# Decoding float64 weights in a fused attention and two-MLP kernel: signs on GpSimd, two VectorE passes in place of three

## The chip, the cores and the metric

The kernel runs on one core of a Trainium2 chip. The metric is device time in microseconds of one execution; lower is better. The core's engines work side by side, each through its own queue in order: TensorE (PE, matrix products into PSUM), VectorE (DVE), ScalarE (ACT), GpSimd (POOL) and SyncE (SP), which issues all the DMAs.

## The reference

Three parts follow each other, here in outline, for 2 sequences of 768 positions. Attention has 8 heads of 64, a causal window of 96 positions beside 8 global ones, and a distance bias. Its output, 512 wide, goes through an MLP with a convolution of 3 taps along the sequence as its gate, and then through an MLP with a spatial product over positions.

```python
x = attention(q, k, v, n_global, n_local)          # (2, 768, 512), fp32
h = relu(x @ w_in)                                 # 512 -> 1024, w_in: float64
h = h * sigmoid(conv3(h, conv_w))                  # conv_w: float64
x = h @ w_out                                      # 1024 -> 512, w_out: float64
h = relu(x @ w_in2)                                # 512 -> 1024, w_in2: float64
u, v = split(h, 2)
v = normalise(v)                                   # over the 512 columns
out = (u * (w_spatial @ v + b_spatial)) @ w_out2   # w_out2: float64
```

The weights w_in, conv_w, w_out, w_in2 and w_out2 are float64, as the scaling by a NumPy float64 in the inputs makes them. q, k, v and w_spatial are worked on as fp32.

## The kernel before

**Weights.** A weight is cut into blocks of 128 partitions by 512 columns: w1 (w_in) and w2 (w_out) have eight each, w3v and w3u (the two halves of w_in2) four each, w4 (w_out2) four. `split_jobs` (line 705) makes one job of a block: load its 512 KB of float64 as pairs of int32 words into a raw buffer (six of them for the first four weights), decode it to fp32 in a wk buffer (four of them), and split that with `parts` (line 558) into a high and a low fp16 half. The high half is a cast on ScalarE (line 496), the low half a subtraction on GpSimd or VectorE (line 510). Every product is then three matmuls of halves: high by high, high by low, low by high.

**Decoding.** `decode` (line 667) has four passes over a block, `hi` and `lo` being the two words of each float64. ScalarE (line 677) reads `hi` as an fp32 number and scales it, which moves the exponent into place. VectorE shifts the result left by three bits (line 684), ORs in the top three bits of `lo` (line 687), and ORs in the sign bit of `hi` (line 692). The convolution's taps, cwt, pass through the same function with 24 columns.

**Other work that bears on the change.** In the attention, line 842 (VectorE) takes scores out of PSUM with their bias and minimum, line 860 (ScalarE) takes the exponentials, line 855 (GpSimd) shifts the minima, and lines 496 and 510 split the probabilities into ph halves. `inner` (line 1034) does the first product (line 1050), relu (1392), the taps (1057, 1063), tanh (1083), the gate (1088) and the split into hh and hl. `outer` (line 1104) does the second product (line 1120) with w2's halves; its result ys is split by lines 494 and 506.

**Order.** The order is made when the kernel is built. `Plan` (line 105) holds every piece of work as a task with a cost for each engine that can do it, some with two engines to choose from, and what it reads and writes. `order` (line 150) lists the tasks by due times, then draws the due times anew `TRIES` times, with a spread, and keeps the shortest plan (lines 173 to 178). The instructions then stand on each engine in that order and can't overtake each other. Up to 70 us of the plan, dummy matmuls (`warm`, line 1019) fill TensorE's gaps. In the present order w1's blocks are decoded from 12 to 50 us, w2's from 50 to 100, w3v's and w3u's up to 160 and w4's around 290.

Of the kernel before, what the change touches and what calls it, by code (L numbers as in the profile page):

```python
# [9 lines left out]
F32 = mybir.dt.float32  # L10
# [4 lines left out]
I32 = mybir.dt.int32  # L15
I64 = mybir.dt.int64
U16 = mybir.dt.uint16
AF = mybir.ActivationFunctionType
ALU = mybir.AluOpType
# [22 lines left out]
VW = 2 * D + 2  # L42
OUT_LO = [0, 254, 510, S]

LEAD_TICKS, LEAD_STEPS = 12, 8

NATS, PLAINS = (0, 1, 2), (0, 1)
# [8 lines left out]

ROUNDS, SLACK, AHEAD, MARGIN, BIAS, CLOSE = 6, 0.5, 60.0, 1.0, 10.0, 15.0

TRIES, SPREAD = 150, 0.7

WARM_TO, WARM_AGAIN = 70.0, 8

# [13 lines left out]
def act(n):  # L76
    return 0.15 + 0.00085 * n
# [298 lines left out]
class Kernel:  # L376
# [287 lines left out]

    def decode(self, f, raw, reads, writes, by=1):

        nc, n = self.nc, f.shape[-1]
        lo, hi, fi = raw[:, :, 0], raw[:, :, 1], f.bitcast(I32)
        base = 2.0**-112 * 2.0 ** {1: 0, 256: 1}[by]

        def scale(e):
            if e == "ACT":
                nc.scalar.activation(out=f, in_=hi.bitcast(F32), func=AF.Copy, scale=base)
            else:
                nc.vector.tensor_scalar(
                    out=f, in0=hi.bitcast(F32), scalar1=base, scalar2=None, op0=ALU.mult  # L680
                )

        def shift(e):
            nc.vector.tensor_scalar(out=fi, in0=fi, scalar1=3, scalar2=None, op0=ALU.logical_shift_left)

        def low(e):
            nc.vector.scalar_tensor_tensor(
                out=fi, in0=lo, scalar=29, in1=fi, op0=ALU.logical_shift_right, op1=ALU.bitwise_or
            )

        def sign(e):
            nc.vector.scalar_tensor_tensor(  # L692
                out=fi, in0=hi, scalar=-(2**31), in1=fi, op0=ALU.bitwise_and, op1=ALU.bitwise_or
            )

        self.plan.add(dict(ACT=act(n)), scale, reads=reads, writes=writes)
        self.plan.add(dict(DVE=0.1 + 0.0008 * n), shift, reads=reads, writes=writes)
        for cost, e in ((0.0014, low), (0.0011, sign)):
            self.plan.add(dict(DVE=0.1 + cost * n), e, reads=reads, writes=writes)
# [5 lines left out]
    def split_jobs(self, weights, raw):  # L705

        jobs = []

        def job(kind, j, src):
            n = self.plan.next(raw)  # L710
            words = self.m(*n).bitcast(I32)
            self.load(words.bitcast(I64), src[:, j], [n], 8 * 512 * P)
            w = self.plan.next("wk")
            f = self.m(*w)[:, :512]
            hi, lo = (part[j] for part in self.blocks(kind))
            name = (kind, 0, j)
            self.decode(f, words.rearrange("p (n t) -> p n t", t=2), [n], [w], 2 ** self.k["w"])
            self.parts(512, hi, lo, f, [w], [(*name, "h")], [(*name, "l")])

        for kind, src in weights:  # L720
            for j in range(src.shape[1]):
                jobs.append(lambda args=(kind, j, src): job(*args))
        return jobs
# [1027 lines left out]
```

## Time and profile before

| | us |
|---|---|
| median of 3 runs | 383.51 |
| the runs | 378.37, 383.51, 384.13 |
| the profiled execution | 378.64 |
| its span, first to last instruction | 376.8 |

| engine | busy us | share of the span |
|---|---|---|
| TensorE | 357.0 | 95% |
| VectorE | 289.2 | 77% |
| ScalarE | 275.0 | 73% |
| GpSimd | 200.4 | 53% |

A busy share is a mean over stages with different limits, so the views that are read for the change are cut by stage. A busy TensorE is not one at its peak: matmuls overlap, and their ends are modelled. Its granted clock is given as a share of 2.4 GHz; the mean over the span is 0.978. Spans on GpSimd are rough.

### The profile page before, as it was taken

The numbers are of one execution on the slowest core, as the hardware profiler recorded it, in microseconds if no ns is written. First come the engines' busy times: TensorE is split into PE (matmuls) and PEld (weight loads), VectorE is DVE, ScalarE is ACT, GpSimd is POOL, SyncE is SP. The second block draws the span as 40 slices with busy tenths as digits, with TensorE's granted clock in tenths as the row PEclk, the third lists the DMA queues.
The fourth block names the chain that finished last, engine by engine and source line by source line (L and its number), as shares of the span: only waits on it lengthen the run. The fifth ranks groups of instructions, "written<-read, shape, count | busy, mean of one in ns | idle before, by whom it ended". The sixth has DMA issues, their size and how long they took to land.

```text
span 376.8 us, 8106 instructions
## 1 busy us (share of the span) xinstructions
PE 357.0 (95%) x2906; PEld 256.1 (68%) x2906; DVE 289.2 (77%) x745; ACT 275.0 (73%) x686; POOL 200.4 (53%) x287
## 2 busy tenths in 40 slices
PE   8999999995879999989999999999999999999994
PEld 5677987773778765666887879887545666664443
DVE  4689999997968898957886787799798897995000
ACT  3899989996737886768988895996788866555221
POOL 4341536759824479746948443779953699000000
PEclk9999999998699999989999999999999999999998
DMA  7966724976383413556422547000234000001222
GB/s 206 408 231 202 275 82 143 283 209 195 72 211 140 121 58 95 104 154 151 93 44 57 108 76 206 2 1 3 53 128 157 14 1 2 0 1 57 104 94 92
DMA packets 46258, 43.64 MB, mean 116 GB/s; under 512 B 34816, under 2 KB 36608, under 8 KB 45696
## 3 DMA queue, kind: packets, MB, share of 16 engines
q1 hardware_dynamic: 46208, 43.03, 40.3%
q8 instruction: 25, 0.41, 0.4%
q14 instruction: 25, 0.20, 0.2%
HBM read 31.48 MB, written 3.15 MB: 92 GB/s over the span
## 4 chain that ended last, share of the span: by engine, by line
PE 55%; DMA 2%; POOL 0%; ACT 0%; issue 0%; ACTq 0%
PE bank L1325 11%; PE bank L1120 9%; PE bank L1050 9%; PE bank L1475 8%; PE bank L1413 7%; PE bank L1204 6%; PE bank L823 2%; DMA pt_dt_float<-ph_dt_float 2%; PE bank L934 1%; PE bank L976 1%; PE bank L935 1%; PE bank L936 1%; PE bank L781 0%; POOL ph_dt_float L510 0%; POOL hl_dt_float L510 0%; ACT sb_dt_float L860 0%
## 5 line engine op out<-in xcount | busy, mean ns | idle before, releaser
L1050 PE MATMUL bank<-x_dt_float,w1h_dt_float 128*128 128x260 f16 (+1 forms) x384 | 64.8, 273 | 0.0
L1120 PE MATMUL bank<-hh_dt_float,w2l_dt_float 128*128 128x254 f16 (+2 forms) x192 | 53.9, 281 | 2.5 <-POOL w2l_dt_float L510 2.5
L1120 PE MATMUL bank<-hl_dt_float,w2h_dt_float 128*128 128x254 f16 (+2 forms) x192 | 53.9, 281 | 1.9 <-POOL hl_dt_float L510 1.2
L1120 PE MATMUL bank<-hh_dt_float,w2h_dt_float 128*128 128x254 f16 (+2 forms) x192 | 54.0, 281 | 1.2 <-DVE ys_dt_float L506 0.9
L1050 PE MATMUL bank<-x_dt_float,w1l_dt_float 128*128 128x260 f16 (+1 forms) x192 | 52.3, 273 | 0.0
L1063 DVE SCALAR_TENSOR_TENSOR bank<-hp_dt_float,cwt,bank 128x254 f32<-128x254 f32 (+2 forms) x96 | 45.7, 485 | 7.7 <-ACT bank L1057 4.9
L510 POOL TENSOR_TENSOR ph_dt_float<-sb_dt_float,ph_dt_float 128x512 f16<-128x512 f32 x30 | 36.3, 1211 | 21.2 <-ACT ph_dt_float L496 9.2
L510 POOL TENSOR_TENSOR hl_dt_float<-ac_dt_float,hh_dt_float 128x254 f16<-128x254 f32 (+2 forms) x47 | 34.2, 741 | 22.1 <-ACT hh_dt_float L496 16.2
L1120 PEld LDWEIGHTS <-w2h_dt_float 128*128 128x128 f16 x384 | 36.7, 100 | 9.5 <-issue 3.2
L842 DVE CUSTOM_DVE_ANT_0 sb_dt_float<-bank,bias_dt_float 128x256 f32<-128x256 f32 (+1 forms) x96 | 35.1, 400 | 9.1 <-PE bank L823 4.5
L1050 PEld LDWEIGHTS <-w1h_dt_float 128*128 128x128 f16 x384 | 36.9, 97 | 5.7 <-issue 0.7
L860 ACT ACTIVATE sb_dt_float<-sb_dt_float,nb_dt_float 128x256 f32<-128x256 f32 (+1 forms) x64 | 29.1, 492 | 3.9 <-POOL nb_dt_float L855 3.0
L1413 PE MATMUL bank<-ys_dt_float,w3uh_dt_float 128*128 128x384 f16 x128 | 31.2, 326 | 0.0
L1475 PE MATMUL bank<-w4h_dt_float,g_dt_float 128*128 128x512 f16 (+1 forms) x104 | 28.9, 363 | 0.0
L1204 PE MATMUL bank<-w3vh_dt_float,ys_dt_float 128*128 128x512 f16 x96 | 28.6, 379 | 0.0
L1475 PEld LDWEIGHTS <-g_dt_float 128*128 128x128 f16 x156 | 15.2, 98 | 15.8
L1325 PE MATMUL bank<-ws_dt_float,vn_dt_float 128*128 128x384 f16 x144 | 25.0, 326 | 0.0
L692 DVE SCALAR_TENSOR_TENSOR wk_dt_float<-raw_dt_float,wk_dt_float 128x512 int32<-128x512 int32 x28 | 24.9, 894 | 0.1
L1120 PEld LDWEIGHTS <-w2l_dt_float 128*128 128x128 f16 x192 | 19.3, 101 | 8.0 <-POOL w2l_dt_float L510 2.8
L1204 PEld LDWEIGHTS <-ys_dt_float 128*128 128x128 f16 x144 | 13.8, 98 | 15.8
L494 ACT ACTIVATE wk_dt_float<-bank 128x512 f32<-128x512 f32 (+1 forms) x13 | 7.3, 564 | 21.7 <-PE bank L1475 21.7
L1057 ACT ACTIVATE bank<-hp_dt_float,cwt 128x254 f32<-128x254 f32 (+2 forms) x48 | 22.5, 478 | 0.0
(186 smaller groups left out, 995.3 us busy)
## 6 DMA issues: line engine op xcount, KB each, us to landing
raw_dt_float<-in_w SPq DMA_DIRECT2D x20, 512.0 KB, 5.7
qk_dt_float<-in_qk SPq DMA_DIRECT2D x24, 336.0 KB, 3.4
v_dt_float<-in_vb SPq DMA_DIRECT2D x4, 1024.0 KB, 6.0
out_x<-wk_dt_float SPq DMA_DIRECT2D x11, 256.0 KB, 2.0
raw_dt_float<-in_wst SPq DMA_DIRECT2D x6, 384.0 KB, 3.7
raw_dt_float<-in_w3v SPq DMA_DIRECT2D x4, 512.0 KB, 4.3
raw_dt_float<-in_w3u SPq DMA_DIRECT2D x4, 512.0 KB, 3.8
v_dt_float<-in_vb SPq DMA_DIRECT2D x2, 768.0 KB, 6.2
```

What stands on the lines that cost most here:

```text
L510: self.engines[e].tensor_tensor(out=out, in0=in0, in1=in1, op=ALU.subtract)
L692: nc.vector.scalar_tensor_tensor(out=fi, in0=hi, scalar=-(2**31), in1=fi, op0=ALU.bitwise_and, op1=ALU.bitwise_or)
L842: nc.vector.tensor_tensor_reduce(out=sb[:, h, :n], in0=self.ps(self.sp[s][h])[:, :n], in1=self.m("bias", 2 * p + h)[:, t0 : t0 + n], scale ...
L860: nc.scalar.activation(out=sb[:, h, :n], in_=sb[:, h, :n], func=AF.Exp, scale=-1.0, bias=nb[:, h : h + 1])
L1050: nc.tensor.matmul(self.ps(acc)[:, :nx], w[f][:, k * P : (k + 1) * P], x[:, k, x0:], start=k == n == 0, stop=k == 3 and n == 2,)
L1057: nc.scalar.activation(out=ac(), in_=near(1), func=AF.Copy, scale=tap(1))
L1063: nc.vector.scalar_tensor_tensor(out=ac(), in0=near(j), scalar=tap(j), in1=ac(), op0=ALU.mult, op1=ALU.add)
L1120: nc.tensor.matmul(ps(), w[2 * d + k // 4][:, k % 4 * P : (k % 4 + 1) * P], x, start=k == n == 0, stop=k == 7 and n == 2,)
L1204: nc.tensor.matmul(ps(), x[:, y, k, tk], w[k], start=n == 0, stop=n == 11)
L1325: self.nc.tensor.matmul(self.ps(acc)[:, :HS], v[:, k, x, ek], w[:, k, y], start=n == 0, stop=n == 8)
L1413: nc.tensor.matmul(ps(), w[e4][:, k * P : (k + 1) * P], x[:, y, k, s], start=n == 0, stop=n == 11)
L1475: nc.tensor.matmul(ps(), x[:, y, k, tk], w[k][:, at], start=n == 0, stop=n == 11)
```

## The change

The blocks of w1, w2, w3v and w3u go through a new function, `decode_beside`. The pass of ScalarE stays. After it, GpSimd multiplies `hi` as fp32 by zero, in place, which leaves a zero with the sign of the number: a word with the sign bit alone. VectorE then has two passes instead of three. The first shifts `lo` right by 29 bits and ORs it with that word, in place of `lo`; the second shifts ScalarE's result left by three and ORs it with that. w4, cwt and the wide fallback keep the old function. The planner's number of draws goes from 150 to 60.

```diff
+BESIDE = ("w1", "w2", "w3v", "w3u")
...
-TRIES, SPREAD = 150, 0.7
+TRIES, SPREAD = 60, 0.7
...
+    def decode_beside(self, f, raw, reads, writes, by):
+        nc, n = self.nc, f.shape[-1]
+        lo, hi, fi = raw[:, :, 0], raw[:, :, 1], f.bitcast(I32)
+        base = 2.0**-112 * 2.0 ** {1: 0, 256: 1}[by]
+        size = hi.bitcast(F32)
+
+        def signs(e):
+            nc.gpsimd.tensor_scalar(out=size, in0=size, scalar1=0.0, scalar2=None, op0=ALU.mult)
+
+        def low(e):
+            nc.vector.scalar_tensor_tensor(
+                out=lo, in0=lo, scalar=29, in1=hi, op0=ALU.logical_shift_right, op1=ALU.bitwise_or
+            )
+
+        def joined(e):
+            nc.vector.scalar_tensor_tensor(
+                out=fi, in0=fi, scalar=3, in1=lo, op0=ALU.logical_shift_left, op1=ALU.bitwise_or
+            )
+
+        self.plan.add(
+            dict(ACT=act(n)), lambda e: nc.scalar.activation(out=f, in_=size, func=AF.Copy, scale=base), reads=reads,
+            writes=writes,
+        )
+        self.plan.add(dict(POOL=0.2 + 0.0019 * n), signs, writes=reads)
+        self.plan.add(dict(DVE=0.1 + 0.0014 * n), low, writes=reads)
+        self.plan.add(dict(DVE=0.1 + 0.0012 * n), joined, reads=reads, writes=writes)
...
-            self.decode(f, words.rearrange("p (n t) -> p n t", t=2), [n], [w], 2 ** self.k["w"])
+            decode = self.decode_beside if kind in BESIDE and self.half else self.decode
+            decode(f, words.rearrange("p (n t) -> p n t", t=2), [n], [w], 2 ** self.k["w"])
```

## Rows read from the trace of the kernel before

**Rows 1.** The page: busy us, share, instructions of each engine; then the dummy matmuls.
```profile
PE 357.0 (95%) x2906; PEld 256.1 (68%) x2906; DVE 289.2 (77%) x745; ACT 275.0 (73%) x686; POOL 200.4 (53%) x287
...
L1021 PE MATMUL bank<-hl_dt_float 128*128 128x256 f16 x84 | 12.9, 299 | 1.2 <-DVE hl_dt_float L578 1.2
```

**Rows 2.** Windows by stage: busy us and instructions of each engine, TensorE's granted clock.
```profile
core 0: us, PE busy (x) PEld busy (x) DVE busy (x) ACT busy (x) POOL busy (x), PEclk, DMA share, GB/s
...
10.00:50.00 40.00, 38.63 (x305) 31.77 (x303) 34.74 (x115) 35.56 (x86) 14.46 (x20) 1.00 0.73 264
50.00:84.00 34.00, 33.48 (x283) 26.76 (x281) 32.56 (x93) 32.21 (x84) 20.97 (x29) 1.00 0.68 188
84.00:105.00 21.00, 14.78 (x143) 11.65 (x142) 17.57 (x31) 15.37 (x37) 18.47 (x19) 0.76 0.54 142
105.00:160.00 55.00, 51.67 (x484) 38.21 (x481) 46.16 (x120) 39.04 (x93) 34.41 (x49) 1.00 0.46 118
...
170.00:285.00 115.00, 114.57 (x1073) 87.04 (x1070) 93.25 (x236) 95.53 (x249) 77.07 (x112) 1.00 0.33 77
```

**Rows 3.** Windows of 10 us around TensorE's largest hole, same columns.
```profile
80.00:90.00 10.00, 6.39 (x62) 4.95 (x59) 9.72 (x18) 8.35 (x20) 6.71 (x5) 1.00 0.79 203
90.00:100.00 10.00, 7.40 (x44) 5.15 (x45) 7.31 (x11) 7.17 (x17) 9.02 (x12) 0.53 0.31 97
100.00:110.00 10.00, 8.01 (x118) 7.22 (x116) 6.48 (x16) 5.24 (x15) 5.40 (x8) 0.95 0.97 193
```

**Rows 4.** What TensorE waited for: us in total, times, the longest.
```profile
PE bank L1120 <- POOL w2l_dt_float L510: 2.5, 1, 2.5
PE bank L781 <- DVE nm_dt_float L842: 1.5, 1, 1.5
```

**Rows 5.** Timeline from 83 us: start, us, engine, line, operation; idle before, and releaser.
```profile
83.33 2.25 DVE L692 SCALAR_TENSOR_TENSOR wk_dt_float<-raw_dt_float,wk_dt_float 128x512 int32<-128x512 int32 x2
...
83.48 1.54 POOL L510 TENSOR_TENSOR ph_dt_float<-sb_dt_float,ph_dt_float 128x512 f16<-128x512 f32 x1 [2.81 <-issue]
...
86.52 2.85 DVE L506 SCALAR_TENSOR_TENSOR vl_dt_float<-v_dt_float,vh_dt_float 128x2048 f16<-128x2048 f32 x1
...
87.18 4.32 POOL L510 TENSOR_TENSOR w2l_dt_float<-wk_dt_float,w2h_dt_float 128x512 f16<-128x512 f32 x2
...
90.44 0.28 PE L1120 MATMUL bank<-hh_dt_float,w2l_dt_float 128*128 128x254 f16 x1 [2.50 <-POOL w2l_dt_float L510]
```

**Rows 6.** The decoding's VectorE passes by line: ns min/median/max, first and last start.
```profile
L684 DVE TENSOR_SCALAR wk_dt_float<-wk_dt_float x28: 407/417/1481, 12.6 to 296.9; 128x512 int32<-128x512 int32 x28
...
L687 DVE SCALAR_TENSOR_TENSOR wk_dt_float<-raw_dt_float,wk_dt_float x28: 657/682/1434, 13.1 to 297.3; 128x512 int32<-128x512 int32 x28
...
L692 DVE SCALAR_TENSOR_TENSOR wk_dt_float<-raw_dt_float,wk_dt_float x28: 673/682/1682, 16.2 to 298.5; 128x512 int32<-128x512 int32 x28
```

**Rows 7.** Windows of lines 684, 687, 692 in that order: VectorE's busy us (passes).
```profile
10.00:50.00 40.00, 6.05 (x11) 1.00 0.73 264
50.00:105.00 55.00, 6.45 (x9) 0.91 0.62 170
...
10.00:50.00 40.00, 6.22 (x10) 1.00 0.73 264
50.00:105.00 55.00, 6.45 (x8) 0.91 0.62 170
...
10.00:50.00 40.00, 6.30 (x9) 1.00 0.73 264
50.00:105.00 55.00, 7.43 (x8) 0.91 0.62 170
```

**Rows 8.** GpSimd passes near the new one: ns min/median/max, and timeline of a memset.
```profile
L510 POOL TENSOR_TENSOR w2l_dt_float<-wk_dt_float,w2h_dt_float x8: 1152/1158/3204, 52.6 to 101.0; 128x512 f16<-128x512 f32 x8
...
2.51 0.25 POOL L839 MEMSET sb_dt_float<- 128x192 f32 x1
```

**Rows 9.** Waits around the raw buffers: SyncE's queue: us in total, times, the longest.
```profile
SPq L554 <- DVE wk_dt_float L692: 50.2, 16, 8.4
```

## The prediction

> **What bounds the kernel now.** I read the busy shares of the page first. TensorE is busy 357.0 of 376.8 us, so no change to other engines can bring more than the 19.8 us that it idles, plus what it loses to a low clock and to dummy matmuls [rows 1]. Next I cut the span into stages with the window view. The reader is to see that the three stages from 10 to 105 us differ from the rest: VectorE and ScalarE are busy 67.3 and 67.8 of the 74 us from 10 to 84, 91% each, while from 170 to 285 us TensorE idles 0.4 of 115 [rows 2]. In the early stages the tasks that run on either engine (copies out of PSUM, relus, casts) tie the two together: the pair is the bound there, and TensorE has holes. Some are filled with dummy matmuls, 12.9 us in the whole run [rows 1].
>
> The largest hole lies from 80 to 110 us: TensorE idles 3.6, 2.6 and 2.0 us in those three tens, and in the middle one its granted clock is 0.53, that is most of it at 1.2 instead of 2.4 GHz, which costs about (1 - 0.53) x 7.4 = 3.5 us [rows 3]. The wait view names two waits there, 1.5 us for a VectorE result (line 842) and 2.5 us for GpSimd's low half of a w2 block (line 510) [rows 4]. The timeline shows how both arise. Two third passes of the decoding (line 692) take 2.25 us beside a GpSimd pass that began 0.15 us after them. Then a long VectorE pass and two GpSimd passes of w2's low halves overlap: the latter take 4.32 us, and TensorE waits for them until 90.44 [rows 5]. So the decoding sits in the bound stage, and VectorE and GpSimd hold each other up.
>
> **What goes.** A block's decoding is now one ScalarE pass and three VectorE passes of 128x512. The medians are 417, 682 and 682 ns, 1.78 us together, and the longest passes take more than twice as long [rows 6]. What lies above the median is waiting, and it follows GpSimd's load. From 10 to 50 us GpSimd is busy 14.46 of 40 us (36%), and from 50 to 105 us 39.4 of 55 (72%) [rows 2]. The windows of the three lines give, per pass (the small passes of cwt, 1.13, 0.17 and 0.17 us, taken out of the first), 4.92/10 = 0.49, 6.05/9 = 0.67 and 6.13/8 = 0.77 us at 36%, and 6.45/9 = 0.72, 6.45/8 = 0.81 and 7.43/8 = 0.93 at 72% [rows 7]. A block costs 1.93 us in w1's stretch and 2.46 in w2's.
>
> **What comes on VectorE.** Two passes with two SBUF inputs each, a strided output in the first. The trace shows no such output; the nearest rows are lines 687 and 692, with the same size and strided inputs. Below, two passes at their minima take 657 + 673 ns = 1.33 us; above, both at their maxima take 1434 + 1682 ns = 3.12 us [rows 6]. I take them at these lines' price under GpSimd's new load. Per block that is 0.67 + 0.77 = 1.44 at 36% and 0.81 + 0.93 = 1.74 at 72%, so 0.3 more for 36 points of load.
>
> **What comes on GpSimd.** One pass of 128x512 f32 in place, with a stride of two words. Nearest rows: the subtractions of w2l, with two inputs, 1.15 us at least and 1.16 at the median; a memset of 128x192 at 0.25 us, which is 0.67 us for 512 [rows 8]. I take 1.1 us, near the former, since it reads and writes. Eight for w1 add 8.8 us to 14.5 of 40 (36% to 58%); eight for w2 add 8.8 to 39.4 of 55 (72% to 88%). By the slope above, a new block's two VectorE passes cost 1.44 + 0.18 = 1.62 in w1's stretch and 1.74 + 0.13 = 1.87 in w2's. Saved: 8 x (1.93 - 1.62) + 8 x (2.46 - 1.87) = 2.5 + 4.7 = 7.2 us of VectorE before 105 us. The ends of this term: at the minima 8 x 0.60 + 8 x 1.13 = 13.8 us saved, at the maxima 8 x 1.19 + 8 x 0.66 = 14.8 us lost.
>
> The two third passes at 83.33 needed 2.25 us with a GpSimd pass beside them, where one needs 673 ns at best [rows 5, 6]. Taken to its end, each added pass holds one VectorE pass up in full: 16 x 1.1 = 17.6 us of VectorE against the clean saving of 13.8, a loss of 3.8 us, 1.9 us of time if the pair shares it. A rule of the Trainium skill says just this, against the change: in "SBUF — State Buffer", section Who interferes with whom, a VectorE instruction with two SBUF inputs and a GpSimd instruction that reads SBUF exclude each other, and the later one waits for the whole of the earlier. The trace agrees for the pair at 83.33, and not as a price of every pass, since the medians stand near the minima (682 against 657 and 673 ns) [rows 6]. So I keep the slope for the sum and the full hold-up for a rival.
>
> **From engine time to time.** VectorE and ScalarE are equally full and share tasks, so 7.2 us off the one is 3.6 us off the pair. TensorE's work after 105 us moves up by as much, since there it is nearly always busy. The eight blocks of w3v and w3u lie from 105 to 160 us, where TensorE is busy 51.7 of 55 us [rows 2]: I count nothing. What hides them is the convolution's matmuls; without that cover they would bring about half of the 4.7 us that w2's eight save on VectorE, 2.4 us. The four blocks of w4 and cwt keep the old decoding.
>
> **Waits and queues.** The new GpSimd pass waits for the ScalarE pass, since it overwrites what that reads. In GpSimd's queue stand behind it the subtractions for hl, ph and the weights' low halves, and the small nb, for which ScalarE's exponentials wait. The first VectorE pass waits for GpSimd; behind it stand lines 842 and 1063, for which ScalarE and TensorE wait. Behind ScalarE's pass a block is decoded after 1.1 + 1.62 = 2.7 us instead of 1.93, if no queue is in the way. SyncE's loads into raw already wait for line 692 (50.2 us over 16 waits) [rows 9]; 0.8 us more per block lies within the six raw buffers, and I cost it at nothing. If the buffers did not cover it, 16 x 0.8 = 13 us spread over six buffers would be 2.1 us.
>
> **The search.** All costs in the plan change, so the whole order is drawn anew, with 60 draws where there were 150. No row shows what a draw is worth. I bound it by a stall like the one from 84 to 90 us: one more or one less, 1.5 + 2.5 + 3.5 = 7.5 us. My value is nothing.
>
> **The sum.** The profiled execution took 378.64 us: 378.64 - 3.6 = 375.0. The runs shown lie in two places, 378.4 and 384, and the median of 383.51 is 4.9 above the profiled one. I lay the forecast half of that, 2.4 us, above the sum: 377.4, rounded to 377. The kernel before, on the same footing, is 381.0.
>
> **Rivals.**
> *The stall goes as well.* With fewer VectorE passes around 82 to 90 us the two waits and the low clock behind them vanish: 375.0 - 7.5 + 2.4 = 370. For it: the decoding stands in front of the first of them [rows 5]. Against: the second is GpSimd's, which gets more to do.
> *Nothing gained.* The hold-ups between GpSimd and VectorE eat the saving, or ScalarE hands no work over and its 91% stay the bound: 378.6 + 2.4 = 381, and with every added pass holding one up in full 383. The Trainium skill's section named above would have it at the latter. For it: third passes at over a microsecond in w2's stretch [rows 5]. Against: the medians.
> *GpSimd's queue becomes the bound, slower.* From 50 to 105 us GpSimd goes from 72% to 88% by my price, and from 84 to 105 us it is already busy 18.47 of 21 [rows 2]. If low halves of w2, hl or ph come later there, TensorE takes another stall like that at 87.9, with the low clock behind it: 378.6 + 7.5 + 2.4 = 388.5. It decides once GpSimd is over some 90% busy in that stretch, that is if the new pass costs 1.3 us rather than 1.1. Against: the subtractions can go to VectorE, and the plan knows the price.
>
> **How the numbers follow.** Forecast 0.45 (377, itself from 373 to 381), stall gone 0.2, nothing gained 0.15, slower 0.2. The range from 368 to 389 leaves out about a third of the second case and somewhat under half of the last. Faster by over 2%, about what a measurement of this kernel can tell from no change, means under 373.4 against 381.0: most of the second case and a tenth of the first, with a little for the search, 0.28. Slower means over 388.6: half of the last case, and some for a worse draw of the order, 0.17. Within: 0.55.
>
> **What would show it.** Right: VectorE's groups of the decoding at 24 x 1.6 to 1.9 us plus w4's; GpSimd's new group x24 at 1.0 to 1.2 us; VectorE's sum down by about 10 us, GpSimd's up by 26; the stage in which TensorE reaches full load begins 3 to 4 us earlier. Wrong: a new pass of 1.5 us or more; passes of the decoding at 1.0 us or more; new TensorE waits for GpSimd (lines 510 and 855) followed by a granted clock near 0.5; or TensorE's idle time moved to places that have nothing to do with decoding, which would make it the search.

## The result and the profile after

The changed kernel took 383.29 us (median of 4 runs, 381.16 to 386.13) and the kernel before 380.94 us (4 runs, 377.85 to 384.13): 1.0136 times the time before, with a 95% interval from 1.0094 to 1.0177. It is about 1.4% slower, 5.2 us, where 377 against 381 was forecast. Ratios compare undisturbed executions only, so they need not be the quotient of the medians beside them.

The profiled execution took 386.13 us, the longest of the four. Line numbers move by 2 to 32: 678 is the new sign pass, 681 and 686 are VectorE's two passes, 512, 715, 874, 887, 966, 1082 and 1152 are the old 510, 684, 842, 855, 934, 1050 and 1120. The page's busy times:

```profile
PE 360.6 (94%) x2887; PEld 254.4 (66%) x2887; DVE 287.0 (75%) x719; ACT 274.9 (72%) x688; POOL 243.7 (63%) x309
```

Against [rows 1] GpSimd has 43.3 us more, and VectorE only 2.2 us less. Its decoding passes of 512 columns fell by 7.2 us (from 62.1 to 54.9), so the rest of its work grew by 5.0. The new passes, by line (ns min/median/max, first and last start):

```profile
L678 POOL TENSOR_SCALAR raw_dt_float<-raw_dt_float x24: 1545/1582/2046, 16.4 to 206.5; 128x512 f32<-128x512 f32 x24
L681 DVE SCALAR_TENSOR_TENSOR raw_dt_float<-raw_dt_float x24: 679/815/1646, 18.0 to 220.0; 128x512 int32<-128x512 int32 x24
L686 DVE SCALAR_TENSOR_TENSOR wk_dt_float<-wk_dt_float,raw_dt_float x24: 678/922/1645, 19.0 to 221.6; 128x512 int32<-128x512 int32 x24
```

The sign pass never took less than 1.545 us. The windows by stage (the columns of [rows 2]):

```profile
10.00:50.00 40.00, 34.95 (x236) 26.27 (x235) 29.69 (x85) 30.40 (x72) 30.25 (x26) 0.93 0.75 260
50.00:84.00 34.00, 30.59 (x253) 24.02 (x251) 29.68 (x74) 28.78 (x71) 27.95 (x34) 0.98 0.31 103
84.00:105.00 21.00, 19.34 (x207) 14.52 (x207) 19.09 (x54) 17.28 (x42) 18.48 (x22) 0.92 0.73 181
170.00:285.00 115.00, 109.83 (x929) 80.77 (x929) 88.52 (x200) 87.91 (x230) 74.98 (x94) 0.99 0.26 63
```

TensorE's idle time moved. From 84 to 105 us it shrank from 6.2 to 1.7 us, but from 10 to 50 us it grew from 1.4 to 5.1, from 50 to 84 from 0.5 to 3.4, and from 170 to 285 from 0.4 to 5.2 us. From 10 to 50 us GpSimd's load went from 14.46 to 30.25 us. Three windows of 10 us hold the largest of the new holes:

```profile
40.00:50.00 10.00, 6.24 (x37) 4.54 (x36) 8.28 (x17) 7.23 (x16) 10.00 (x8) 0.71 0.49 159
...
80.00:90.00 10.00, 7.07 (x47) 4.27 (x47) 8.19 (x19) 7.81 (x19) 10.00 (x10) 0.83 0.63 163
...
200.00:210.00 10.00, 7.41 (x70) 6.09 (x69) 7.48 (x21) 6.24 (x18) 6.08 (x6) 0.83 0.64 103
```

In the first two GpSimd has no free moment (10.00 of 10). In the first, TensorE idled from 41.6 to 45.4 us, and from 44.5 to 51 us its granted clock was 0.50, that is 1.2 instead of 2.4 GHz. TensorE's longest waits (us, times, longest), where [rows 4] had 2.5 us for GpSimd and 1.5 for line 842; the last row is the second wait in the kernel before:

```profile
PE bank L1082 <- DVE nm_dt_float L874: 6.9, 3, 3.8
PE bank L966 <- DMA pt_dt_float<-ph_dt_float: 5.2, 3, 2.6
...
PE bank L934 <- DMA pt_dt_float<-ph_dt_float: 3.7, 2, 2.0
```

The first wait names VectorE. The timeline of each engine shows what VectorE had waited for (GpSimd, then VectorE, then TensorE):

```profile
37.95 1.15 POOL L512 TENSOR_TENSOR w1l_dt_float<-wk_dt_float,w1h_dt_float 128x512 f16<-128x512 f32 x1
39.05 1.26 POOL L1000 COPY x_dt_float<-x_dt_float 128x16 f16<-128x16 f16 x2
40.29 2.01 POOL L678 TENSOR_SCALAR raw_dt_float<-raw_dt_float 128x512 f32<-128x512 f32 x1
42.25 3.83 POOL L512 TENSOR_TENSOR w1l_dt_float<-wk_dt_float,w1h_dt_float 128x512 f16<-128x512 f32 x3
...
42.33 1.63 DVE L681 SCALAR_TENSOR_TENSOR raw_dt_float<-raw_dt_float 128x512 int32<-128x512 int32 x1 [1.47 <-POOL raw_dt_float L678]
43.88 1.12 DVE L715 TENSOR_SCALAR cwt<-cwt 128x24 int32<-128x24 int32 x1
44.92 0.41 DVE L874 CUSTOM_DVE_ANT_0 sb_dt_float<-bank,bias_dt_float 128x256 f32<-128x256 f32 x1
...
45.39 0.59 PE L1082 MATMUL bank<-x_dt_float,w1h_dt_float 128*128 128x256 f16 x2 [3.77 <-DVE nm_dt_float L874]
```

The sign pass stands in GpSimd's queue behind a subtraction and a copy. VectorE's first pass waits 1.47 us for it. Behind that pass stand the shift of the taps (line 715) and the scores of line 874, and TensorE waits 3.77 us for these. The queue is only part of this wait. Three subtractions follow the sign pass on GpSimd, and beside them VectorE's pass takes 1.63 us, where its minimum is 0.68, and the shift of 24 columns takes 1.12 us, as it did before; in an order below in which no such hold-up falls on it, it takes 0.17.

The second hole has the same form (GpSimd, then VectorE, then TensorE):

```profile
79.71 1.58 POOL L678 TENSOR_SCALAR raw_dt_float<-raw_dt_float 128x512 f32<-128x512 f32 x1
81.24 1.39 POOL L887 TENSOR_TENSOR nb_dt_float<-nm_dt_float,shift 128x2 f32<-128x2 f32 x1
82.59 1.15 POOL L512 TENSOR_TENSOR ph_dt_float<-sb_dt_float,ph_dt_float 128x512 f16<-128x512 f32 x1
...
83.78 0.42 DVE L874 CUSTOM_DVE_ANT_0 sb_dt_float<-bank,bias_dt_float 128x256 f32<-128x256 f32 x1 [1.19 <-POOL ph_dt_float L512]
...
84.26 0.38 PE L1082 MATMUL bank<-x_dt_float,w1h_dt_float 128*128 128x260 f16 x2 [2.52 <-DVE nm_dt_float L874]
```

A sign pass, the shift of the minima and a subtraction of the probabilities follow each other on GpSimd. VectorE's scores wait 1.19 us for the subtraction, and TensorE 2.52 us for the scores. So an engine that is off the path decides when its neighbours may start.

The third hole has no sign pass in its chain:

```profile
194.42 1.16 POOL L512 TENSOR_TENSOR ph_dt_float<-sb_dt_float,ph_dt_float 128x512 f16<-128x512 f32 x1
...
195.61 9.03 DMA pt_dt_float<-ph_dt_float
...
204.69 0.23 PE L966 MATMUL bank<-vh_dt_float,pt_dt_float 128*128 128x65 f16 x1 [2.59 <-DMA pt_dt_float<-ph_dt_float]
```

The transposition of the probabilities was issued at 195.61 us, as the subtraction before it ended, and took 9.03 us to land, where the median of the 16 is 5.1. Three loads of w3u's blocks, 512 KB each, had been issued from 192.34 us on. That they are what slowed it is likely and not shown.

### The profile page after: what moved, and what is told of

Its sections match the earlier page's. It is cut to its first block, busy times and chain, and to the rows that moved or that the text cites. A ratio compares the mean times of both kernels' runs of the same rounds, so it can differ in the third digit from the quotient of the medians.

```text
span 384.3 us, 8056 instructions
## 1 busy us (share of the span) xinstructions
PE 360.6 (94%) x2887; PEld 254.4 (66%) x2887; DVE 287.0 (75%) x719; ACT 274.9 (72%) x688; POOL 243.7 (63%) x309
## 4 chain that ended last, share of the span: by engine, by line
PE 71%; DMA 10%; POOL 8%; DVE 5%; issue 2%; ACT 2%; SPq 0%; DVEq 0%; POOLq 0%; ACTq 0%
PE bank L1082 13%; PE bank L1357 11%; PE bank L1152 9%; PE bank L1507 8%; PE bank L1445 8%; PE bank L1236 8%; DMA pt_dt_float<-ph_dt_float 5%; PE bank L960 4%; PE bank L855 4%; DMA v_dt_float<-in_vb 3%; POOL ph_dt_float L512 2%; POOL raw_dt_float L678 2%; PE bank L905 1%; PE bank L966 1%; POOL nb_dt_float L887 1%
## 5 line engine op out<-in xcount | busy, mean ns | idle before, releaser
L1082 PE MATMUL bank<-x_dt_float,w1h_dt_float 128*128 128x260 f16 (+1 forms) x384 | 69.7, 284 | 6.9 <-DVE nm_dt_float L874 6.9
L1082 PE MATMUL bank<-x_dt_float,w1l_dt_float 128*128 128x260 f16 (+1 forms) x192 | 54.5, 284 | 1.1 <-POOL w1l_dt_float L512 1.1
L1152 PE MATMUL bank<-hh_dt_float,w2h_dt_float 128*128 128x254 f16 (+2 forms) x192 | 52.5, 273 | 1.4 <-DVE xk_dt_float L977 1.2
L1152 PE MATMUL bank<-hh_dt_float,w2l_dt_float 128*128 128x254 f16 (+2 forms) x192 | 52.4, 273 | 1.0 <-POOL w2l_dt_float L512 0.9
L1152 PE MATMUL bank<-hl_dt_float,w2h_dt_float 128*128 128x254 f16 (+2 forms) x192 | 52.3, 272 | 0.1
L512 POOL TENSOR_TENSOR ph_dt_float<-sb_dt_float,ph_dt_float 128x512 f16<-128x512 f32 x32 | 40.1, 1259 | 9.3 <-ACT ph_dt_float L498 8.8
L678 POOL TENSOR_SCALAR raw_dt_float<-raw_dt_float 128x512 f32<-128x512 f32 x24 | 41.1, 1718 | 6.6 <-ACT wk_dt_float L691 6.6
L874 DVE CUSTOM_DVE_ANT_0 sb_dt_float<-bank,bias_dt_float 128x256 f32<-128x256 f32 (+1 forms) x96 | 35.1, 402 | 11.3 <-PE bank L855 4.0
L681 DVE SCALAR_TENSOR_TENSOR raw_dt_float<-raw_dt_float 128x512 int32<-128x512 int32 x24 | 23.2, 976 | 5.0 <-POOL raw_dt_float L678 5.0
L1424 ACT ACTIVATE hp_dt_float<-bank 128x260 f32<-128x260 f32 (+1 forms) x48 | 18.2, 384 | 10.8 <-PE bank L1082 8.8
L686 DVE SCALAR_TENSOR_TENSOR wk_dt_float<-wk_dt_float,raw_dt_float 128x512 int32<-128x512 int32 x24 | 23.7, 1005 | 0.0
```

Source lines behind the costliest of these rows:

```text
L512: self.engines[e].tensor_tensor(out=out, in0=in0, in1=in1, op=ALU.subtract)
L678: nc.gpsimd.tensor_scalar(out=size, in0=size, scalar1=0.0, scalar2=None, op0=ALU.mult)
L686: nc.vector.scalar_tensor_tensor(out=fi, in0=fi, scalar=3, in1=lo, op0=ALU.logical_shift_left, op1=ALU.bitwise_or)
L874: nc.vector.tensor_tensor_reduce(out=sb[:, h, :n], in0=self.ps(self.sp[s][h])[:, :n], in1=self.m("bias", 2 * p + h)[:, t0 : t0 + n], scale ...
L1082: nc.tensor.matmul(self.ps(acc)[:, :nx], w[f][:, k * P : (k + 1) * P], x[:, k, x0:], start=k == n == 0, stop=k == 3 and n == 2,)
L1152: nc.tensor.matmul(ps(), w[2 * d + k // 4][:, k % 4 * P : (k % 4 + 1) * P], x, start=k == n == 0, stop=k == 7 and n == 2,)
```

## Experiments

**The passes by themselves.** A kernel that does nothing else runs each pass four times alone, then GpSimd's and VectorE's side by side.

```python
def signs():   g.tensor_scalar(out=size, in0=size, scalar1=0.0, scalar2=None, op0=ALU.mult)   # 2-word stride, in place
def packed():  g.tensor_scalar(out=fa, in0=fa, scalar1=0.0, scalar2=None, op0=ALU.mult)
def minus():   g.tensor_tensor(out=fb, in0=fa, in1=fb, op=ALU.subtract)
def blank():   g.memset(size, 0.0)
def low():     v.scalar_tensor_tensor(out=blo, in0=blo, scalar=29, in1=bhi, op0=ALU.logical_shift_right, op1=ALU.bitwise_or)
```

> The passes by themselves, on one block: only these passes and the copies are run, the rest of the work is left out. Forms of a GpSimd pass over 128x512, four of each: the change's (fp32 times zero, every second word, in place), the same on packed words, from every second word to packed, from packed to every second word, a subtraction with two inputs, a memset of every second word. Then the two VectorE passes and the old shift alone, then VectorE passes beside GpSimd passes. If the stride makes the pass long: 1.5 to 1.6 us for the change's form and about 1.1 for the packed one. If a one-input fp32 pass on GpSimd simply costs that: all forms with an input at 1.5 or more. If the two engines exclude each other only while GpSimd reads: VectorE's two-input passes rise from 0.68 to over 1.5 us beside the multiplication and stay at 0.68 beside the memset; the shift, with one input, is then held up or not by the same row.

Its timeline (start, us of the group; alone first, then VectorE's passes beside four of GpSimd's: low beside signs, the old shift, line 79, beside signs, low beside memsets, low beside subtractions):

```profile
4.96 6.38 POOL L50 TENSOR_SCALAR raw_a<-raw_a 128x512 f32<-128x512 f32 x4 [4.52 <-DMA raw_a<-in_w]
11.30 6.21 POOL L53 TENSOR_SCALAR fa<-fa 128x512 f32<-128x512 f32 x4
...
30.21 5.28 POOL L62 TENSOR_TENSOR fb<-fa,fb 128x512 f32<-128x512 f32 x4
35.44 2.36 POOL L65 MEMSET raw_a<- 128x512 f32 x4
...
38.08 2.87 DVE L68 SCALAR_TENSOR_TENSOR raw_b<-raw_b 128x512 int32<-128x512 int32 x4
...
43.88 1.81 DVE L79 TENSOR_SCALAR fc<-fc 128x512 int32<-128x512 int32 x4
...
46.40 6.83 POOL L50 TENSOR_SCALAR raw_a<-raw_a 128x512 f32<-128x512 f32 x4
...
45.69 10.09 DVE L68 SCALAR_TENSOR_TENSOR raw_b<-raw_b 128x512 int32<-128x512 int32 x12
...
65.93 10.52 DVE L79 TENSOR_SCALAR fc<-fc 128x512 int32<-128x512 int32 x16
...
76.44 5.77 DVE L68 SCALAR_TENSOR_TENSOR raw_b<-raw_b 128x512 int32<-128x512 int32 x8
...
82.25 9.55 DVE L68 SCALAR_TENSOR_TENSOR raw_b<-raw_b 128x512 int32<-128x512 int32 x8
```

The multiplication by zero takes about 1.5 us alone, packed (6.21 us for four) as with a stride (6.38), while the subtraction with its two inputs takes 1.3 us with fp32 output. My nearest row was not near: fewer inputs did not make it cheaper. Side by side, twelve VectorE passes take 10.09 us where they would take 8.6 alone (12 x 2.87 / 4), so four sign passes cost VectorE 1.5 us, 0.37 us each. Four subtractions cost it 9.55 - 5.74 = 3.8 us, 0.95 each, and four memsets nothing (5.77). The expectation of over 1.5 us for each pass beside a multiplication missed. The old shift, with one input, is held up as well: sixteen take 10.52 us instead of 7.24, which is 0.82 us for each sign pass.

**GpSimd's pass and VectorE's saving, each alone, in the order before.** The edits don't touch the plan, so every other instruction keeps its place. The VectorE pass that is left out takes 0.68 us in the median. The change itself puts two passes of 1.36 us together, at best, in place of three of 1.78, which is 0.42 less; so the third kernel is kinder to the trade than the change.

```diff
# before_load and before_both: one more GpSimd pass per block, behind ScalarE's
+            if by == 256 and n == 512 and words[0] in BESIDE:
+                same = hi.bitcast(F32)
+                nc.gpsimd.tensor_scalar(out=same, in0=same, scalar1=1.0, scalar2=None, op0=ALU.mult)
# before_nolow and before_both: the pass with the low bits is left out for the same 24 blocks
-            nc.vector.scalar_tensor_tensor(
+            if by == 1 or words[0] not in BESIDE:
+                nc.vector.scalar_tensor_tensor(
```

> The kernel before in its own order, with a GpSimd pass more for each of the 24 blocks, right behind ScalarE's: fp32 times one, in place, on the high words, so nothing computed changes. VectorE keeps its three passes, the last of which reads what GpSimd wrote. If GpSimd's added time is what costs (its queue, and the hold-ups of VectorE): 8 to 15 us slower than before, 1.02 to 1.04. If the other order of the changed kernel is to blame: within 2 us of before, 0.995 to 1.005.

> The kernel before in its own order, with VectorE's pass for the low words left out in the 24 blocks (the weights lose their last three bits of 23): 18 us of VectorE less, nothing more on GpSimd. If VectorE is the bound before 105 us, and ScalarE shares: 3 to 6 us faster, 0.985 to 0.992. If the order on the engines, or ScalarE, holds the time: within 2 us, 0.995 to 1.005.

> Both edits at once, in the order of the kernel before: a GpSimd pass more and a VectorE pass less for each of the 24 blocks, which is the trade of the change without its new order. If the trade loses by itself: 4 to 10 us slower, 1.01 to 1.025. If the new order is what loses: between 3 us faster and no change, 0.99 to 1.002.

| kernel | ratio to before | interval |
|---|---|---|
| GpSimd pass added | 1.0382 | 1.0355 to 1.0409 |
| VectorE pass left out | 0.983 | 0.9795 to 0.9864 |
| both | 1.0217 | 1.0145 to 1.0289 |

The two multiply to 1.0206: they add up. Leaving out a VectorE pass took 17.8 us off that engine (271.4 busy against 289.2) and about 6.5 us off the time, so VectorE was worth having. But the added pass put 38.1 us on GpSimd and cost some 14.5 us. The windows of the kernel with the added pass show how full GpSimd's queue gets where [rows 3] had the hole:

```profile
90.00:100.00 10.00, 5.88 (x46) 4.77 (x46) 8.11 (x14) 6.56 (x14) 10.00 (x8) 0.83 0.57 184
100.00:110.00 10.00, 3.35 (x33) 2.56 (x33) 5.74 (x8) 6.15 (x14) 10.00 (x13) 0.55 0.17 53
```

TensorE is busy 3.35 of 10 us while GpSimd works through, and one wait for the low half of h took 5.3 us. What stands behind in GpSimd's queue comes late elsewhere too. ScalarE's exponentials wait 11.3 us in all for the shifted minima where they waited 3.0 in the kernel before (us, times, longest; the kernel before first):

```profile
ACT sb_dt_float L860 <- POOL nb_dt_float L855: 3.0, 5, 1.5
...
ACT sb_dt_float L860 <- POOL nb_dt_float L855: 11.3, 8, 4.6
```

Part of the cost is VectorE held up: it is busy 298.0 us instead of 289.2, for the same instructions; half of that, by the prediction's rule, would be 4.4 of the 14.5 us.

**The length of the sign pass, in the changed kernel's order.** Here the plan is the changed kernel's, and only the pass is cut: to 8 columns, to 352 columns (about the length that the plan assumes), or replaced by memsets, which read nothing. In all of them VectorE's first pass takes a sign from a bit of the low word instead (in the two cut ones together with the sign of the first column), in one instruction of the same kind over as many elements, so the true signs and the low bits are left out.

```diff
# after_cut8; after_cut352 has 352 for 8 on GpSimd's line
-            nc.gpsimd.tensor_scalar(out=size, in0=size, scalar1=0.0, scalar2=None, op0=ALU.mult)
+            nc.gpsimd.tensor_scalar(out=size[:, :8], in0=size[:, :8], scalar1=0.0, scalar2=None, op0=ALU.mult)
-                out=lo, in0=lo, scalar=29, in1=hi, op0=ALU.logical_shift_right, op1=ALU.bitwise_or
+                out=lo, in0=lo, scalar=31, in1=hi[:, 0:1].to_broadcast([P, n]), op0=ALU.logical_shift_left, op1=ALU.bitwise_xor
# after_memset; after_memset3 has three of them; VectorE's line takes bit 0 or bit 31 of the low word
+            nc.gpsimd.memset(size, 0.0)
```

> The changed kernel as it is, beside the three that follow, which keep its order of instructions on every engine. 1.01 to 1.02 of before.

> The changed kernel in its own order, GpSimd's pass cut from 512 columns to 8, so that all that waits for it still does but it takes some 0.1 us instead of 1.72. The weights' signs are taken from the low words' last bit instead (their values are as large as before, the output is another). If the length of GpSimd's pass is what costs: 8 to 13 us faster than the changed kernel, 0.98 to 0.99 of before. If the new order itself is worse, whatever the pass takes: 0 to 3 us faster than the changed kernel, 1.005 to 1.015 of before.

> The same with 352 of the 512 columns, about 1.1 to 1.2 us, the time that the plan and the prediction had for the pass. If the mis-sized pass turned the gain into a loss: about 0.99 to 1.0 of before, most of the way to the cut to 8 columns. If its length matters little: 1.01 of before. If any reading pass on GpSimd costs as such, through the hold-ups: halfway, 1.0 to 1.01.

> The changed kernel in its own order, with a memset of the same 512 high words to zero on GpSimd in place of the multiplication: the same words written, nothing read. The signs come from the low words' last bit. If VectorE is held up only by GpSimd passes that read SBUF: VectorE's two passes fall from about 1.0 us to about 0.9 or less, and the time falls to 0.985 to 0.995 of before, also because the memset is shorter. If a memset takes as long as the multiplication and holds VectorE up as well: 1.01.

> The changed kernel in its own order; in place of the multiplication three memsets of the same 512 high words, about 0.57 us each by the run with one, so 1.6 to 1.7 us of GpSimd as in the change, but nothing read. The signs come from a mantissa bit instead (values as large as before, the output is another). If GpSimd's time in its queue is what costs: as slow as the changed kernel, 1.007 to 1.017 of before. If VectorE's being held up by a reading GpSimd pass is what costs: like the cut to 8 columns, 0.98 to 0.995, with both VectorE passes at a median under 0.70 us. Between them, 0.995 to 1.007: both take part.

| sign pass | its median, us | ratio to before | interval |
|---|---|---|---|
| 8 columns | 0.24 | 0.9881 | 0.9774 to 0.9988 |
| 352 columns | 1.15 | 1.0086 | 1.0047 to 1.0126 |
| whole (the changed kernel again) | 1.59 | 1.0125 | 1.0088 to 1.0161 |
| three memsets | 3 x 0.57 | 1.0222 | 1.0142 to 1.0303 |

The passes by line in the kernels with 8 columns, 352 columns and three memsets:

```profile
L681 DVE SCALAR_TENSOR_TENSOR raw_dt_float<-raw_dt_float x24: 677/691/1647, 17.3 to 214.8; 128x512 int32<-128x512 int32 x24
L686 DVE SCALAR_TENSOR_TENSOR wk_dt_float<-wk_dt_float,raw_dt_float x24: 677/694/1664, 18.2 to 216.5; 128x512 int32<-128x512 int32 x24
```
```profile
L678 POOL TENSOR_SCALAR raw_dt_float<-raw_dt_float x24: 1133/1154/1614, 15.8 to 202.2; 128x352 f32<-128x352 f32 x24
L681 DVE SCALAR_TENSOR_TENSOR raw_dt_float<-raw_dt_float x24: 676/881/1656, 17.3 to 214.5; 128x512 int32<-128x512 int32 x24
```
```profile
L678 POOL MEMSET raw_dt_float<- x72: 548/568/602, 15.8 to 207.2; 128x512 f32 x72
L681 DVE SCALAR_TENSOR_TENSOR raw_dt_float<-raw_dt_float x24: 680/686/1646, 17.7 to 216.7; 128x512 int32<-128x512 int32 x24
```

In one order, the time grows with the length of GpSimd's pass: 2.4% from 0.24 to 1.59 us, of which 2.05% come before 1.15 us. The three memsets read no SBUF, and the VectorE pass behind them is at its clean 686 ns in the median, but the loss is at least as large. So it doesn't take a sign pass that reads beside VectorE: its time in GpSimd's queue suffices. The hold-ups don't vanish with the memsets, though. The second VectorE pass has a median of 970 ns there, since it comes to lie beside GpSimd's subtractions, and VectorE's two passes cost 1.99 us a block as in the changed kernel (1.98). With 8 columns they still cost 1.83. So the runs don't part the delay in the queue from the hold-ups by the subtractions that the queue moves. VectorE's busy sum puts a size on the latter: 282.3 us with 8 columns, 287.2 with the whole pass, 4.9 us of which half, by the prediction's rule, would be 2.5 of the 9.3 us of time. The two waits for line 874 follow the pass: 3.77 and 2.52 us in the changed kernel's profile, 3.36 and 1.57 with 352 columns, 2.42 and 1.21 with 8, 3.58 and 2.69 with three memsets. More than half of the first is there with 8 columns too, so the pass's length doesn't make that part.

With the single memset the run says nothing: w_out's low words end in zeros, so all its signs came out positive, the kernel took its wide fallback, and that lasts 1742 us.

**The order and its price.** A pass of 1.58 us stands in the plan at 1.17 (0.2 + 0.0019 x 512). Four kernels give the plan 1.68, others start the draws from another number, and one shows what a redrawn order does to the saving of a VectorE pass (it leaves the low bits' pass out of the plan too). The change from 150 to 60 draws does nothing: drawn with 150, the changed kernel's instructions stand in the very same order on every engine. The changed kernel's orders from the second and third number are drawn 150 times, those with the true price 60 times; drawn equally often (60 times for the second number, 150 for the third), both would have the very orders that ran.

```diff
# after_priced; priced_seed2 and priced_seed3 with Random(2) and Random(3) as well
-        self.plan.add(dict(POOL=0.2 + 0.0019 * n), signs, writes=reads)
+        self.plan.add(dict(POOL=0.2 + 0.0029 * n), signs, writes=reads)
# after_seed2, after_seed3 (with TRIES 150), before_seed2, before_seed3; Random(3) for the third number
-        draw = random.Random(1)
+        draw = random.Random(2)
# short_plan, on the kernel before
-        for cost, e in ((0.0014, low), (0.0011, sign)):
+        for cost, e in ((0.0011, sign),) if words[0] in BESIDE else ((0.0014, low), (0.0011, sign)):
# priced_w1, with the price of 0.0029
-BESIDE = ("w1", "w2", "w3v", "w3u")
+BESIDE = ("w1",)
```

> The changed kernel with the plan's cost of GpSimd's pass at 1.68 us (0.2 + 0.0029 x 512) instead of 1.17; the order is drawn anew. If the plan's wrong price put the pass in bad places: 0.99 to 1.0 of before. If GpSimd's time can't be hidden in any order of this plan: 1.005 to 1.02.

> The changed kernel with another start of the draws, so the same work in another order (the plan's 150 draws keep another best). If the order decides: off from 1.013 of before by more than 0.007, either way. If the work decides: 1.006 to 1.02.

> The kernel before with VectorE's pass for the low words left out of the plan as well, for the same 24 blocks (the weights lose the last three of 24 bits; GpSimd gets nothing more); the order is drawn anew. If the gain of 6 to 7 us seen in the old order carries over: 0.975 to 0.985 of before. If the new order matters as much as the work: anywhere from 0.965 to 1.0.

> The kernel before with its 150 draws started from another number, same work. Theory A (the changed kernel's loss is the sign pass's time in GpSimd's queue, with a wrong price in the plan): the orders of the kernel before scatter by about half a per cent and this lies within 0.995 to 1.005, so the changed kernel's two orders (1.0125 and 1.007) are slower than it as a whole. Rival B (the loss is a lucky order before and a common one after): 1.007 to 1.015.

> As before_seed2, with a third number. Theory A: 0.995 to 1.005. Rival B: 1.007 to 1.015, the same range in which the changed kernel's orders lie.

> The changed kernel in a third order, same work. Theory A: 1.005 to 1.015 like the first two. Rival B: between 0.995 and 1.015, with a spread as wide as that between kernels.

> The changed kernel with the sign pass priced at 0.2 + 0.0029 n in the plan (1.68 us), and the order drawn from the second number. Theory A: 0.995 to 1.003, like the first order drawn with that price (1.0009), and below the same number's order with the planned price (1.007). Rival B: the price is no cause, and it lies at 1.005 to 1.015 as often as not.

> The changed kernel with the true price of the sign pass and the third number's order. Theory A with the price as a cause of its own: below the same number's order with the planned price (1.020), at 1.000 to 1.010, so that the three priced orders lie lower than the three others one by one. Rival B (the price is no cause): 1.010 to 1.020.

> The sign pass with its true price for w1's eight blocks alone, in whose stretch GpSimd was busy 36% and the pair of VectorE and ScalarE 91%; all other blocks are decoded as before. If the pass pays where GpSimd has slack: 0.985 to 0.997. If the pass costs as much there as it saves: 0.997 to 1.008, inside the scatter of orders.

| draws from | kernel before | changed kernel | changed, with the true price |
|---|---|---|---|
| 1 | 1 | 1.0125 (1.0088 to 1.0161) | 1.0009 (0.9981 to 1.0036) |
| 2 | 1.002 (0.9991 to 1.0048) | 1.0072 (1.0034 to 1.011) | 1.0077 (1.0044 to 1.011) |
| 3 | 0.9957 (0.9925 to 0.9988) | 1.0198 (1.0141 to 1.0255) | 1.0022 (0.9976 to 1.0068) |
| mean | 0.9992 | 1.0132 | 1.0036 |

Every order of the changed kernel is slower than every order of the kernel before, three against three, so the 1.4% is hardly the bad luck of one draw. With the true price one order of three lies among those of the kernel before. One order differs from the next by 0.2 to 1.3% with the same work, which is as much as the change was meant to bring. The true price lowered the mean by 1%: two pairs fell by 1.2 and 1.8%, one not at all. Likely the price is a cause of its own, worth up to 1.0 of the 1.4%; three pairs don't settle it. In the three priced orders the granted clock is 1.00 from 10 to 50 us, in the three others 0.93, 0.97 and 0.87.

The redrawn order without the low bits' pass took 0.9953 (0.9911 to 0.9995) where the old order had 0.983: planning for less work gave back most of the gain. VectorE's busy sum fell there by 6.0 us (283.2) and not by 17.8, with 732 instructions where the old order had 721: the plan gave the freed VectorE other work (ScalarE has 8 instructions fewer and GpSimd 5). The sign pass for w1's blocks alone took 1.0088 (1.0057 to 1.0119), so it brought nothing where GpSimd had the most room either; with one order drawn, that much may be its luck.

No version of the sign pass beat the kernel before. Only kernels that drop work did (8 columns, no low bits), and the kernel before in its third order (0.9957).

## Why the prediction was wrong, step by step

**The bound was right.** VectorE's time in the early stages did limit the kernel. Without a GpSimd pass in the way (8 columns) the changed order takes 0.988, 4.5 us less, with an interval from 0.5 to 8.6; the prediction had 3.6 us. Leaving out one pass in the old order is 6.5 us for 17.8 us of VectorE; by the rule used, half of the part before 105 us, it is 16 x 0.74 / 2 = 5.9 [rows 7]. That the saving survives a new order was taken for granted: of the 6.5 us the redrawn one kept 1.8.

**The failed step is GpSimd's term.** The prediction added its 26 us (24 x 1.1) at no cost but a slope on VectorE's passes, and gave the queue behind them to a rival at 0.2. The runs put a price on GpSimd's time, with the hold-ups that come along: 14.5 us for 38.1 us in the old order (0.38 us of time for each us on GpSimd), and 2.4% or 9.3 us for 24 x 1.35 = 32 us in the new one (0.29). Even at the predicted length the change loses, since 352 columns take 1.0086. In the prediction's terms the loss divides into - 4.5 us for VectorE, + 7.8 us for a pass of 1.15 us and + 1.5 us for the rest: 378.6 becomes 383.4, or 1.0127. These terms are read from the same runs, so that they add up is no test of them.

**The pass's length was the smaller error.** 1.1 us was taken from the subtractions, 1.58 us was measured; it is worth 1.5 of the 9.3 us. The prediction set 1.3 us as the point from which GpSimd's queue decides. It decides earlier: at 1.15 us the gain is already gone, in an order that was planned for just such a pass (1.17). Against the rival it also held that the plan knows the price. The plan did not, and three orders drawn with the true price have a mean of 1.0036 instead of 1.0132. So in a new order the length may weigh more than 1.5 us, but not enough there either to bring the forecast gain.

**VectorE saved less than worked out.** The windows of the two lines give 14.9 us for w1's eight blocks and 16.3 for w2's, 1.86 and 2.03 us a block where 1.62 and 1.87 were forecast: 4.0 us saved instead of 7.2. The slope explains part of it. GpSimd was at 76% instead of 58% from 10 to 50 us (30.25 of 40), since the sign passes are longer and ten of them, not eight, fall into that stage, and 1.44 + 0.3 x 40 / 36 = 1.77 at that load. But from 50 to 105 us it gives 1.84 at 84%, and with 8 columns, where GpSimd is at 43 and 74%, it gives 1.50 and 1.76, 1.63 in the mean, where 1.81 us a block was measured. So GpSimd's load is not the whole of it: a pass beside a subtraction pays more than one beside a sign pass (0.95 against 0.37 us).

**The share of a stage was the wrong yardstick for a queue in order.** The rival asked for over 90% on GpSimd between 50 and 105 us. It was 84% there (46.4 of 55), and the first loss fell earlier, at 41 to 45 us, in a stage at 76%. What counts is the stretch of some 10 us in which GpSimd is full, and what stands behind it: line 874 on VectorE (842 before), which the part on waits and queues had listed without a price, and behind it TensorE's line 1082. The other line that it listed, 1063 (now 1095), is in neither chain.

**The blocks that were counted at nothing.** w3v's and w3u's eight were to lie under the convolution's matmuls from 105 to 160 us. The new order decodes them from 160 to 222 us instead, and there is the third hole, in which TensorE waits for a transposition issued behind their loads and not for a sign pass. The order was taken as given, and it is not.

**The search** was rightly held at nothing for the number of draws, and its bound of 7.5 us covers the scatter between orders. **The rivals**: the queue's is what happened, at about two thirds of its price (5.2 us against 7.5). The full hold-up was not: the pairs of passes show 0.37 us for each sign pass, not its whole length. The pair at 83.33 us, from which the prediction took it, had a subtraction beside it, and beside a subtraction the loss is 0.95 us.

## What to carry to other kernels

An engine that is half idle in the mean is not free: work that is put into its queue in order delays all that stands behind it, and here each us on GpSimd cost 0.3 to 0.4 us of time, hold-ups of VectorE included, as much as a us saved on VectorE brought. Before a pass is moved, its cost is to be measured on the engine that gets it, and the chain behind it read from a timeline rather than from a share. Where a plan orders the work, redraw both kernels a few times before a per cent is believed.

## What was unexpected in the hardware

A one-input multiplication on GpSimd took 1.49 to 1.6 us for 128x512 fp32 whatever the stride, more than the two-input subtraction (1.3 us to fp32, 1.15 us to fp16), and a memset 0.56 us. VectorE's one-input shift of that size took 0.43 us. The Trainium skill says of GpSimd, in "GPSIMD Engine Reference", section 4.1 Engine selection, that one-input elementwise work is roughly line-rate and two-input work about twice as slow as on VectorE; the first half differs from these rows, which decide (1.5 us against 0.43), and the second agrees (1.3 us, where VectorE's passes with two inputs take 0.69).

VectorE's passes with two SBUF inputs lost 0.37 us to each sign pass beside them, 0.95 us to each subtraction and nothing to memsets (5.77 us for eight, 5.74 alone). The Trainium skill, in "SBUF — State Buffer", section Who interferes with whom, has the later of two such instructions wait for the whole of the earlier, and none beside one that only writes. The last agrees; the first fits the subtraction better than the multiplication, which held VectorE up for a quarter of its length.
